# Sparse attention with two MLPs: all PSUM as one tile, softmax's maximum and difference over two banks, and split squares in fixed rooms of SBUF

## The chip, the cores and the metric

The kernel runs on one core of one Trainium2 chip. The metric is the device time of one execution in microseconds; lower is better. Three executions of the kernel before took 823.47, 827.84 and 828.2 us (median 827.84).

## The reference

Attention over 4 batches, 8 heads, 576 positions and a head size of 64, in float32. Four heads see only the last 32 positions (local), the other four see every 32nd position (strided). Its result, 2304 tokens by 512 channels, goes through two MLPs with an inner size of 2048.

```python
scores = scale * q @ k.T                      # masked: local for h < 4, strided for h >= 4
attn = exp(scores - max(scores)); attn /= sum(attn) + 1e-9
x = (attn @ v).transpose(0, 2, 1, 3).reshape(2304, 512)
h = x @ w_in;   x = (s * relu(h) ** 2 + b) @ w_out
h = x @ w_in2;  x = where(h >= 1, h, where(h <= -1, 0, (h + 1) ** 2 / 4)) @ w_out2
```

## The kernel before

Every float32 product of the MLPs is done with three matmuls of 384 columns on operands that are split into a high and a low part (`mm3`, lines 859 to 861, and `mm3s`, lines 1102 to 1104): high by high, high by low, low by high. The weights come from HBM in 8-byte words (`raw`, three buffers of 512 KB over 128 partitions), and `decode` and `weights` (L459 to L475) turn each into a high and a low half with two ScalarE and three VectorE or GpSimd operations.

The tokens are worked in six units of 384. Attention is cut into 21 tiles, 12 strided and 9 local ones (`attend`). A tile goes through these steps:

- TensorE writes scores into two PSUM banks (L737 to L757). For the first six tiles (`NACC`) these are two of the four banks named acc; later they are both banks named side.
- VectorE takes the maximum of each bank (L765, two instructions of 256 elements) and subtracts it from each bank (L768, two of 256). ScalarE takes the exponential (L771), VectorE the sum (L772) and its reciprocal (L773), and GpSimd or VectorE multiplies (L774).
- TensorE transposes four 128x128 blocks into a bank named h ("flip", L783); a copy brings them to SBUF as `pt`.
- TensorE multiplies by the values into both side banks (L799 for strided tiles, L809 for local ones). ScalarE moves each bank to the high half `xh` of x (L440), VectorE makes the low half `xl` of it (L842). A tile that crosses a unit's end is cut there, so that one bank takes two or more instructions.

Then, unit by unit, the first half of the first MLP's inner size: `hidden` multiplies `xh` and `xl` by the first weights into bank h, ScalarE and others take relu, the square `t` and its halves `gg`, and `output` multiplies these by the second weights into the four acc banks. The unit's partial sums go to HBM (`part`). The other half of the inner size and the second MLP follow pair of units by pair of units with seven products in place of eight (`product`, `hidden2`, `output2`); the prepared weight quarters go out to HBM from `prepare` and come back as `w0h`, `kb` and others.

No order is written by hand. Every step is recorded as an `Op` with a cost, and `Issue.order` draws 96 orders from the due times plus random jitter (`DRAWS`, `JITTER`) and keeps the one whose end is earliest by its own costs. `AHEAD` is how much earlier than due attention's later tiles are put. The same planner fills expected idle time of TensorE in the first 45 us with throwaway matmuls of 512 bf16 columns ("fills", L731), so many as `busy` is told:

```python
def busy(e, o, out):
    for _ in range(o.fills):
        e.matmul(out=out, lhsT=warm_t[:, 0:out.shape[0]], rhs=warm_t[:, 0:out.shape[1]], start=True, stop=True)
```

Storage is handed out by rings: PSUM tags h (2 banks), side (2) and acc0 to acc3 (1 each); SBUF tags such as `gg` (3 buffers of high and low half side by side), `t` (2) and `pi` (4). The rows of early attention tiles sit in x's tiles of units that are not open yet (`homes`).

Of the kernel before, what the change touches and what calls it, by code (L numbers as in the profile page):

```python
# [24 lines left out]
UMAX = max(UNITS)  # L25
GW = 2 * UMAX + 16
# [14 lines left out]
AHEAD = 3.0  # L41
# [10 lines left out]
PAIRS = NT // (2 * NP)  # L52
KP = DFF // 256
# [51 lines left out]
class Ring:  # L105
    def __init__(self, bufs):
        self.bufs, self.taken, self.made = bufs, [], []
# [220 lines left out]
def sparse_attention_two_mlps(ctx: ExitStack, tc: tile.TileContext, loc, strd, w_ins, w_outs, fixed, out):  # L328
# [17 lines left out]
    part_d = [dr.tile([KD, 128, n], F32, name=f"part_{u}") for u, n in enumerate(UNITS)]  # L346
# [10 lines left out]

    def home(tag):
        ring = rings.setdefault(tag, Ring(1))
        ring.name = tag  # L360
        serial[0] += 1
        name = f"{tag}_{serial[0]}"
        return Buf(ring, lambda: const.tile([128, KD * UMAX], F32, name=name, tag=tag))

    class Tokens:
        def __init__(self, tag):
            self.tag, self.bufs = tag, {}

        def open(self, u):
            tag, n = f"{self.tag}{u}", UNITS[u]  # L370
            ring = rings.setdefault(tag, Ring(1))
            ring.name = tag
            self.bufs[u] = Buf(ring, lambda: const.tile([128, KD, n], F32R, name=tag, tag=tag))
            return self.bufs[u]

        def __getitem__(self, u):
            return self.bufs[u].tile

    xh, xl, opened = Tokens("xh"), Tokens("xl"), {}
# [10 lines left out]

    def split_bufs(z):

        hi = buf(sp, "gg", [128, GW], F32R, LAG + 1)
        whole = hi.make

        def upper():
            hi.both = whole()
            return hi.both[:, UMAX:UMAX + z]

        hi.make = upper  # L400
        ring = rings.setdefault("gl", Ring(LAG + 1))
        ring.name = "gl"
        return hi, Buf(ring, lambda: hi.both[:, 0:UMAX])

    def wide_bank(tag, bufs, shape):
        b = buf(ps, tag, [128, 512], F32, bufs)
        whole = b.make

        def part():
            b.bank = whole()  # L410
            return b.bank[:, 0:shape[0] * shape[1]].rearrange("p (a b) -> p a b", a=shape[0])

        b.make = part
        return b
# [180 lines left out]
    def rows(i):  # L595
# [22 lines left out]
        if i in homes:  # L618
# [7 lines left out]
            else:  # L626
                for j in range(2):
                    load(i, both, [(lambda j=j: row()[:, j], strd[b, 2 * d + j][:, 0:VC])], 128 * VC * 4, 4 * VC)
# [801 lines left out]
```

## Time and profile before

| | |
|---|---|
| three executions | 823.47, 827.84, 828.2 us |
| profiled execution: its time, its span | 825.62 us, 823.7 us |
| TensorE busy | 811.2 us, 98% of the span |
| weight loads, VectorE, ScalarE, GpSimd busy | 785.3, 624.5, 515.1, 109.8 us |
| mean granted TensorE clock | 0.995 of 2.4 GHz |
| moved by DMA | 218.23 MB, 265 GB/s on average |

A matmul's row shows its time from entering to leaving the array, and matmuls overlap; the pace is read from the number of them in a stretch, and a stall from TensorE's idle time. The views used below are the table by stretches, the waits, the groups of instructions and the timeline.

### The profile page before, as it was taken

The page shows a single profiled execution, that of the slowest core. Times are in us where ns is not written, and L with a number is a line of the kernel's source. Part 1 is how long each engine was busy: PE and PEld are TensorE (multiplying, and loading weights), DVE is VectorE, ACT ScalarE, POOL GpSimd, SP SyncE. Part 2 cuts the span into 40 slices and gives each one's busy share as a digit, 9 for nine tenths or more (in the row PEclk, how much of TensorE's full clock was granted, in tenths as well). Part 3 has the DMA queues.
Part 4 walks back from the last instruction along what each step waited for, and adds up shares of the span by engine and source line. Part 5 has one row for each costly group of instructions (what it writes and reads, how often), then busy time and mean ns, then how long its engine had stood idle before and what let it go on. Part 6 is the DMA issues. An engine that isn't in the chain of part 4 may idle for free.

```text
span 823.7 us, 17684 instructions
## 1 busy us (share of the span) xinstructions
PE 811.2 (98%) x6301; PEld 785.3 (95%) x6301; DVE 624.5 (76%) x1314; ACT 515.1 (63%) x1052; POOL 109.8 (13%) x213
## 2 busy tenths in 40 slices
PE   7999999999999999999999999999999999999998
PEld 3689999998999999999999999999999999999998
DVE  4878438887867478679889987997477987466966
ACT  2577446555656566558676677855486855667553
POOL 4032104342321013030221010000000000000000
PEclk9999999999999999999999999999999999999999
DMA  7796355888777468899989999788988889878882
GB/s 230 259 294 203 113 178 196 301 293 288 266 263 253 157 244 279 287 313 341 338 320 326 308 397 342 255 252 281 300 253 255 254 251 294 288 254 253 250 271 95
DMA packets 105523, 218.23 MB, mean 265 GB/s; under 512 B 14196, under 2 KB 27868, under 8 KB 105436
## 3 DMA queue, kind: packets, MB, share of 16 engines
q1 hardware_dynamic: 95196, 180.41, 67.5%
q0 software_dynamic: 10240, 36.71, 11.9%
q8 instruction: 50, 0.82, 0.4%
q14 instruction: 37, 0.30, 0.1%
HBM read 170.93 MB, written 46.14 MB: 264 GB/s over the span
## 4 chain that ended last, share of the span: by engine, by line
PE 96%; DMA 2%; SPq 1%; DVE 0%; ACT 0%; issue 0%; POOL 0%; ACTq 0%
PE acc L1104 8%; PE acc L1103 8%; PE acc L1102 8%; PE h L859 8%; PE h L861 8%; PE h L860 8%; PE side L1104 6%; PE side L1102 6%; PE side L1103 6%; PE acc L859 4%; PE acc L861 4%; PE acc L860 4%; PE h L1104 3%; PE h L1103 3%; PE h L1102 3%; PE side L809 1%
## 5 line engine op out<-in xcount | busy, mean ns | idle before, releaser
L859 PE MATMUL h<-xh,w0h 128*128 128x384 f32 x192 | 65.7, 342 | 0.0
L859 PE MATMUL h<-xh,w0hx 128*128 128x384 f32 x192 | 65.6, 342 | 0.0
L861 PE MATMUL h<-xh,w0lx 128*128 128x384 f32 x192 | 64.6, 337 | 1.0 <-POOL w0lx L475 0.7
L860 PE MATMUL h<-xl,w0hx 128*128 128x384 f32 x192 | 64.4, 336 | 0.0
L860 PE MATMUL h<-xl,w0h 128*128 128x384 f32 x192 | 64.4, 336 | 0.0
L861 PE MATMUL h<-xh,w0l 128*128 128x384 f32 x192 | 64.4, 336 | 0.0
L505 POOL DMA_DIRECT2D dw<-pp x60 | 43.4, 723 | 157.6 <-DVE pp L503 131.0
L886 ACT ACTIVATE t<-h 128x384 f32<-128x384 f32 x50 | 24.5, 489 | 46.6 <-PE h L861 46.3
L898 DVE TENSOR_TENSOR gg<-t,gg 128x384 fp32r<-128x384 f32 x36 | 20.0, 555 | 26.7 <-ACT gg L440 26.7
L861 PEld LDWEIGHTS h<-xh,w0lx 128*128 128x128 f32 x192 | 36.0, 188 | 1.6 <-POOL w0lx L475 1.0
L859 PEld LDWEIGHTS h<-xh,w0h 128*128 128x128 f32 x192 | 36.0, 188 | 0.5
L859 PEld LDWEIGHTS h<-xh,w0hx 128*128 128x128 f32 x192 | 36.0, 188 | 0.5
L860 PEld LDWEIGHTS h<-xl,w0h 128*128 128x128 f32 x192 | 36.1, 188 | 0.0
L860 PEld LDWEIGHTS h<-xl,w0hx 128*128 128x128 f32 x192 | 36.1, 188 | 0.0
L861 PEld LDWEIGHTS h<-xh,w0l 128*128 128x128 f32 x192 | 36.0, 188 | 0.0
L440 ACT ACTIVATE gg<-w1h 128x384 fp32r<-128x384 f32 x48 | 24.9, 523 | 15.9 <-PE acc L1104 6.2
L1148 DVE TENSOR_TENSOR gg<-w1h,gg 128x384 fp32r<-128x384 f32 x48 | 26.5, 556 | 10.5 <-ACT gg L440 10.2
L859 PE MATMUL acc<-gg,w1h 128*128 128x384 f32 (+1 forms) x96 | 33.4, 348 | 0.0
L859 PE MATMUL acc<-gg,w1hx 128*128 128x384 f32 (+1 forms) x96 | 32.6, 340 | 0.0
L861 PE MATMUL acc<-gg,w1l 128*128 128x384 f32 (+1 forms) x96 | 32.3, 336 | 0.0
L861 PE MATMUL acc<-gg,w1lx 128*128 128x384 f32 (+1 forms) x96 | 32.2, 336 | 0.0
L860 PE MATMUL acc<-gg,w1h 128*128 128x384 f32 x96 | 32.2, 335 | 0.0
(607 smaller groups left out, 2804.8 us busy)
## 6 DMA issues: line engine op xcount, KB each, us to landing
dw<-pp POOLq DMA_DIRECT2D x60, 512.0 KB, 5.2
w0h<-dw SPq DMA_DIRECT2D x84, 256.0 KB
w0l<-dw SPq DMA_DIRECT2D x84, 256.0 KB
w0hx<-dw SPq DMA_DIRECT2D x84, 256.0 KB
w0lx<-dw SPq DMA_DIRECT2D x84, 256.0 KB
raw<-in_w_ins SPq DMA_DIRECT2D x32, 512.0 KB
raw<-in_w_outs SPq DMA_DIRECT2D x32, 512.0 KB
kb<-dw SPq DMA_DIRECT2D x56, 256.0 KB
```

Of the source, the lines that this page charges most:

```text
L440: e.activation(out=out, in_=in_, func=AF.Copy)
L505: op(lambda e: e.dma_start(out=dw[o][i][qs].rearrange("q p w n -> p q (w n)"), in_=y.tile[:, 0:nq].bitcast(F32).rearrange("p q w n -> p q ...
L809: e.matmul(out=pv[blk].tile[half(par), hp, c:c + 32], lhsT=v4(pos)[half(blk), s, 2 * hp + par, :], rhs=pt.tile[half(blk), 2 * par + pos, r ...
L859: e.matmul(out=acc, lhsT=wh, rhs=ah, start=first, stop=False)
L860: e.matmul(out=acc[:, 0:al.shape[1]], lhsT=wh, rhs=al, start=False, stop=False)
L861: e.matmul(out=acc, lhsT=wl, rhs=ah, start=False, stop=last)
L886: op(lambda e: e.activation(out=c(t), in_=c(p), func=AF.Relu), [act(n)], [p], [t])
L898: op(lambda e: e.tensor_tensor(out=c(gl), in0=c(t), in1=c(gh).bitcast(F32), op=SUB), [pool(n)] + [dve2(n)], [t, gh], [gl])
L1102: e.matmul(out=dst, lhsT=wh, rhs=ah, start=opens and first, stop=False, skip_group_check=not opens)
L1103: e.matmul(out=dst[:, 0:al.shape[1]], lhsT=wh, rhs=al, start=False, stop=False, skip_group_check=not opens)
L1104: e.matmul(out=dst, lhsT=wl, rhs=ah, start=False, stop=last, skip_group_check=not opens)
L1148: op(lambda e, g=g, hi=hi, lo=lo: e.tensor_tensor(out=lo.tile[:, 0:n], in0=g.tile, in1=hi.tile[:, 0:n].bitcast(F32), op=SUB), [dve2(n)], [ ...
```

## The change

- All eight PSUM banks become one tile, `banks_t`; `bank` hands out banks of it in the same turns as before (acc0 to acc3 are banks 0 to 3, side 4 and 5, h 6 and 7).
- Since a tile's two score banks now lie side by side in one tile (`both`), the maximum is one instruction over two banks (512 elements), and so is the difference. For local tiles both value banks are moved out by one instruction per half.
- x is kept per pair of units and half of the channels ([128, 2, 768]) and not per unit ([128, 4, 384]). Attention's results are cut only where a pair ends. The second MLP's input is read back into these tiles when both units of a pair are done with theirs.
- The halves of the squares (`g_t`) and the squares and partial sums (`f_t`) are fixed rooms near the start of SBUF; before, `t`, `gg` and `pi` were rings near its end. All other tiles move up by 18,624 bytes or less.
- `AHEAD` goes from 3.0 to 4.0, one more tile (10) gets a home in x's tiles, some of the planner's costs are changed, and code for uneven units goes.

```diff
-AHEAD = 3.0
+AHEAD = 4.0
...
+    BANKS = {"acc0": [0], "acc1": [1], "acc2": [2], "acc3": [3], "side": [4, 5], "h": [6, 7]}
+    def bank(tag, *shape):
+        ring = ring_of(("bank", tag), len(BANKS[tag]))
+        def make():
+            b.at = BANKS[tag][ring.used % ring.bufs]
+            ring.used += 1
+            b.bank = banks_t[:, b.at, :]
...
+    def both(two, n):
+        assert two[1].at == two[0].at + 1
+        return banks_t[:, two[0].at:two[0].at + 2, 0:n]
+    def place_in(arena, key, places, n):
+        k = turns.get(key, 0)
+        turns[key] = k + 1
+        a = places[k % len(places)]
+        t = g_t if arena == "g" else f_t
+        b = Part(lambda: t[:, a:a + n])
+        old = [x for x in taken[arena] if x[0] < a + n and a < x[1]]
+        b.writers = list(dict.fromkeys(o for *_, x in old for o in (*x.writers, *x.readers)))
...
     def split_bufs(z):
+        return tuple(place_in("g", v, [i * GW + v * NP for i in range(LAG + 1)], n) for v, n in ((1, z), (0, NP)))
...
-        for par in range(2):
-            op(lambda e, par=par: e.tensor_reduce(out=mx.tile[:, 4 * par:4 * par + 4], in_=sc[par].tile, op=ALU.max,
-                                                  axis=mybir.AxisListType.X), [dve(256)], [sc[par]], part=[mx])
-        for par in range(2):
-            op(lambda e, par=par: e.tensor_tensor(out=fours(2 * par, 2 * par + 2), in0=sc[par].tile.rearrange("p (a b) n -> p a b n", b=2),
-                                                  in1=each(2 * par, 2 * par + 2), op=SUB), [dve(256)], [sc[par], mx], part=[full])
+        op(lambda e: e.tensor_reduce(out=mx.tile.rearrange("p (c a) -> p c a", c=2), in_=both(sc, 256).rearrange("p c (a n) -> p c a n", n=64),
+                                     op=ALU.max, axis=mybir.AxisListType.X), [dve(512)], sc, part=[mx])
+        op(lambda e: e.tensor_tensor(out=sm().rearrange("p (c a) (b n) -> p c a b n", c=2, b=2),
+                                     in0=both(sc, 256).rearrange("p c (a b n) -> p c a b n", a=2, b=2),
+                                     in1=mx.tile.rearrange("p (c a b) -> p c a b", c=2, a=2).unsqueeze(4).to_broadcast([128, 2, 2, 2, 64]),
+                                     op=SUB), [dve(512)], [*sc, mx], part=[full])
...
+            moved_out([(lambda: both(pv, 256).rearrange("p c (h s q) -> p h s c q", h=2, s=4),
+                        lambda w: x_of(w, off, end).rearrange("p h (s c q) -> p h s c q", c=2, q=32))], pv, 512, 0.00104)
...
-        for u in us:
-            begun = op(lambda e: None, [("none", 0.0, 0.0)], after=[x_last[u]], allocs=[x2[u]])
+        begun = op(lambda e: None, [("none", 0.0, 0.0)], after=[x_last[u] for u in us], allocs=[x2[p, 0], x2[p, 1]])
```

How the order moves, at three places. First VectorE, its first instructions after the set-up of constants: the maximum (TENSOR_REDUCE mx from a bank) and the difference (TENSOR_TENSOR sm) of the first two tiles, the sum (mx from sm) and the reciprocal. Before:

```order
L765 TENSOR_REDUCE mx_201<-acc_17_199 128x4
L765 TENSOR_REDUCE mx_201<-acc_16_198 128x4
L768 TENSOR_TENSOR sm_200<-acc_16_198,mx_201 128x2x128
L768 TENSOR_TENSOR sm_200<-acc_17_199,mx_201 128x2x128
L765 TENSOR_REDUCE mx_235<-acc_25_233 128x4
L765 TENSOR_REDUCE mx_235<-acc_24_232 128x4
L772 TENSOR_REDUCE mx_201<-sm_200 128x8
L768 TENSOR_TENSOR sm_234<-acc_24_232,mx_235 128x2x128
L768 TENSOR_TENSOR sm_234<-acc_25_233,mx_235 128x2x128
L773 RECIPROCAL mx_201<-mx_201 128x8
```

The same place in the changed kernel:

```order
L785 TENSOR_REDUCE mx_187<-banks_t 128x8
L787 TENSOR_TENSOR sm_186<-banks_t,mx_187 128x4x128
L785 TENSOR_REDUCE mx_218<-banks_t 128x8
L793 TENSOR_REDUCE mx_187<-sm_186 128x8
L787 TENSOR_TENSOR sm_217<-banks_t,mx_218 128x4x128
L794 RECIPROCAL mx_187<-mx_187 128x8
L795 TENSOR_TENSOR sm_186<-sm_186,mx_187 128x4x128
```

Each pair has become one instruction; their sequence is otherwise kept.

Second TensorE, around the scores of the first local tile (number 3, whose rows come in last among those of the first tokens). Before, behind the last of its score matmuls (L757) stand tile 1's flip (L783) and then tile 0's values (L799, alternately into the two side banks):

```order
L757 MATMUL acc_40_338<-xl_9_281 32x64
L757 MATMUL acc_41_339<-xl_9_281 32x64
L783 MATMUL h_384<-id_t,sm_234 128x128 x4
L799 MATMUL side_392<-pt_323,w0hx_195 64x54 x2
L799 MATMUL side_393<-pt_323,w0hx_195 64x54 x2
```

In the changed kernel tile 0's values (L820) stand behind tile 2's scores (L763) and ahead of the local tile's, which begin with the mask (L758):

```order
L763 MATMUL banks_t<-k_4_206,q_5_209 54x54 x2
L763 MATMUL banks_t<-k_4_206,q_5_209 36x36 x2
L763 MATMUL banks_t<-k_4_206,q_5_209 54x54 x6
L820 MATMUL banks_t<-pt_271,w0hx_183 64x54 x16
L758 LDWEIGHTS idb_t
L758 MATMUL banks_t<-bias_t,idb_t 128x256
```

The values of tile 0 have moved from behind the first local tile's scores to ahead of them.

Third TensorE, after the first matmuls of `hidden` on unit 0. Before, 24 of them (two blocks of 128 inner values) are followed by three fills (the last is shown here), tile 5's flip, four more fills (the first is shown) and tile 5's values:

```order
L731 LDWEIGHTS warm_t
L731 MATMUL h_815<-warm_t 128x512
L783 MATMUL h_815<-id_t,sx_703 128x128 x4
L731 LDWEIGHTS warm_t
L731 MATMUL side_835<-warm_t 128x512
```

In the changed kernel 33 of them stand ahead of that flip (the last is the first row here), three behind it, and then two fills (the first is shown) and the values:

```order
L868 MATMUL banks_t<-xh_166,w0l_473 128x384
L804 MATMUL banks_t<-id_t,sx_629 128x128 x4
L866 MATMUL banks_t<-xh_166,w0h_472 128x384
L867 MATMUL banks_t<-xl_167,w0h_472 128x384
L868 MATMUL banks_t<-xh_166,w0l_473 128x384
L752 LDWEIGHTS warm_t
L752 MATMUL banks_t<-warm_t 128x512
```

A third block of `hidden` has moved ahead of tile 5's values, and five fills are gone there. Over the whole program TensorE has 46 fills and not 53, VectorE 1,236 instructions and not 1,316, ScalarE 1,040 and not 1,054; the 4,248 matmuls of 384 or 386 columns and attention's other matmuls are as many as before. From the end of attention on, TensorE's matmuls come in the same sequence of blocks in both.

## Rows read from the trace of the kernel before

**Rows 1.** Cores: span and mean granted TensorE clock, of full speed.

```profile
core 0: 823.7 us, clock 0.995
```

**Rows 2.** Stretches: length; PE, weight loads, DVE, ACT, POOL busy; clock; DMA share; GB/s.

```profile
0.00:37.46 37.46, 30.72 (x588) 18.09 (x588) 22.81 (x65) 14.11 (x36) 10.08 (x45) 0.91 0.75 244
37.46:44.86 7.40, 7.40 (x107) 6.22 (x100) 6.80 (x15) 4.84 (x10) 1.83 (x2) 1.00 0.98 301
44.86:80.00 35.14, 34.14 (x355) 31.34 (x350) 29.64 (x69) 26.75 (x62) 11.73 (x20) 1.00 0.83 254
80.00:220.00 140.00, 138.75 (x1817) 130.04 (x1816) 95.88 (x239) 77.11 (x172) 41.78 (x76) 1.00 0.67 226
220.00:480.00 260.00, 260.00 (x1493) 259.66 (x1492) 205.15 (x419) 171.40 (x337) 41.64 (x67) 1.00 0.83 289
...
520.00:820.20 300.20, 300.20 (x1730) 299.90 (x1728) 228.91 (x439) 188.66 (x374) 0.00 (x0) 1.00 0.81 255
820.20:823.74 3.54, 0.02 (x1) 0.00 (x0) 0.56 (x1) 0.03 (x1) 0.00 (x0) 0.86 0.31 111
```

**Rows 3.** TensorE's waits: us in total, times, longest; 0 to 45, then after.

```profile
PE acc L757 <- DMA xh<-in_loc: 2.3, 1, 2.3
PE acc L757 <- DMA xl<-in_loc: 1.9, 1, 1.9
PE side L731 <- DVE xl L842: 0.8, 1, 0.8
...
PE h L783 <- issue: 1.2, 1, 1.2
```

**Rows 4.** Groups on VectorE by shape: busy us, mean ns, idle before.

```profile
L765 DVE TENSOR_REDUCE mx<-side 128x4 f32<-128x256 f32 x30 | 11.4, 417 | 8.0 <-PE side L757 4.7 <-PE side L742 3.3
L772 DVE TENSOR_REDUCE mx<-sm 128x8 f32<-128x520 f32 x14 | 9.7, 690 | 0.9 <-ACT sm L771 0.8
```

**Rows 5.** Timeline, 8 to 38 us: start, duration, engine, line, instruction, count.

```profile
8.67 1.90 PE L731 MATMUL acc<-warm_t 128*128 128x512 bf16 x8
8.84 0.76 DVE L765 TENSOR_REDUCE mx<-acc 128x4 f32<-128x256 f32 x2
...
19.20 1.12 PE L799 MATMUL side<-pt,w0hx 54*64 54x54 f32 x32
20.25 2.74 PE L731 MATMUL h<-warm_t 128*128 128x512 bf16 x6
...
30.91 0.66 ACT L440 ACTIVATE xh<-side 128x256 fp32r<-128x256 f32 x2 [1.40 <-PE side L809]
31.33 0.76 DVE L842 TENSOR_TENSOR xl<-side,xh 128x256 fp32r<-128x256 f32 x2 [0.66 <-ACT xh L440]
...
35.84 0.89 DVE L842 TENSOR_TENSOR xl<-side,xh 128x128 fp32r<-128x128 f32 x4 [0.29 <-ACT xh L440]
...
37.47 0.44 PE L859 MATMUL h<-xh,w0h 128*128 128x384 f32 x1
```

**Rows 6.** Timeline, 41.7 to 68.1 us, the same columns.

```profile
41.74 0.82 PE L731 MATMUL h<-warm_t 128*128 128x512 bf16 x3
42.40 0.60 PE L783 MATMUL h<-id_t,sx 128*128 128x128 f32 x4
42.84 1.03 PE L731 MATMUL side<-warm_t 128*128 128x512 bf16 x4
43.79 0.67 PE L809 MATMUL side<-pt,qx 64*64 64x32 f32 x32
...
44.86 0.44 PE L859 MATMUL h<-xh,w0h 128*128 128x384 f32 x1
...
61.63 0.44 PE L861 MATMUL h<-xh,w0lx 128*128 128x384 f32 x1 [0.32 <-DVE w0lx L475]
...
68.04 0.44 PE L861 MATMUL h<-xh,w0lx 128*128 128x384 f32 x1 [0.69 <-POOL w0lx L475]
```

More of the change, by code (lines that the diff above doesn't have):

```diff
@@ L720, in attend @@
         ahead = i < NACC
-        sc = [wide_bank(f"acc{i % 2 * 2 + par}" if ahead else "side", 1 if ahead else 2, [4, 64]) for par in range(2)]
+        sc = [bank(f"acc{i % 2 * 2 + par}" if ahead else "side", 4, 64) for par in range(2)]
         tag = ("sm", "sm", "sx")[i % 3]
@@ L789, in attend @@
         nv = 108 if strided else 128
-        pv = [wide_bank("side", 2, [2, nv]) for _ in range(2)]
+        pv = [bank("side", 2, nv) for _ in range(2)]
         def values(e, i=i):
@@ L870, in hidden @@
     def hidden(g, u, whole=None):
-        n = UNITS[u]
-        p = buf(ps, "h", [128, UMAX], F32, 2)
+        t0, n = (NP * u, NP) if whole else (U0[u], UNITS[u])
+        p, more = bank("h", n), 0
         if whole:
-            t, own = whole, [whole]
+            t = whole
         else:
-            t = buf(sp, "t", [128, UMAX], F32, TB)
             more = 2 * (u == COUNTED)
-            gh, gl = split_bufs(UMAX + more)
-            own = [t, gh, gl]
+            gh, gl = split_bufs(n + more)
+            t = square_buf()
         w = wt[g, 0]
         for k in range(KD):
-            pe_op(lambda e, k=k: mm3(e, p.tile[:, 0:n], cut(w, k), (xh[u][:, k, :], xl[u][:, k, :]), k == 0, k == KD - 1),
-                  n, [*w, x_buf[u][k]], [p], own if k == 0 else ())
-        x_last[u] = chain[0]
+            pe_op(lambda e, k=k: mm3(e, p.tile, cut(w, k), (x_at("h", k, t0, n), x_at("l", k, t0, n)), k == 0, k == KD - 1),
+                  n, [*w, *(x_buf[v][k] for v in range(NU) if t0 < U0[v + 1] and U0[v] < t0 + n)], [p], [whole] if whole and k == 0 and whole.ring else ())
+        if whole:
+            x_last[u] = chain[0]
         c = lambda b: b.tile[:, 0:n]
@@ L904, in units @@
     def units(hi, lo, n):
[L905 removed]
+        op(lambda e: copy(e, hi.tile[:, n:n + 2], ones_t[:, 0:2]), [("pool", 0.2, 0.1)], part=[hi], after=hi.writers)
     bias_sum = Buf(None, None)
@@ L930, in output @@
         z = n + 2 * (u == COUNTED)
[L931 to L937 removed]
+        gh, gl = gt
+        cg = lambda: (gh.tile[:, 0:z], gl.tile[:, 0:n])
         for c in range(KD):
             if opens:
[L940 removed]
+                acc[c] = bank(f"acc{c}", z)
             a = acc[c]
@@ L1002, in inputs @@
[L1002 to L1009 removed]
+            whose = [x2[p, int(place[1]) - 1]]
@@ new lines, in inputs @@
+            op(lambda e, place=place, b=b: copy(e, b.tile[:, 0], x(place)), [("act", 0.17 + 2 * NP * 0.00062, 0.1)], [quarter[p][place], *whose], [b],
+               after=[x_last[i // 2 * 2], x_last[i // 2 * 2 + 1], *(mixed if i < 2 else ())] if i < NB else plan.ops[begin:])
+            op(lambda e, place=place, b=b: e.tensor_tensor(out=b.tile[:, 1], in0=x(place), in1=b.tile[:, 0].bitcast(F32), op=SUB),
+               [("dve", 0.09 + 2 * NP * 0.00104, 0.1, "port")], [quarter[p][place], *whose], [b])
```

268 lines of the change are left out of this document (98 added, 170 removed).

## The prediction

> **What bounds the kernel now.** I read the cores first, then the table by stretches, TensorE's waits, the groups of VectorE and last the timeline where TensorE is not steady. TensorE's clock is granted at 0.995 of 2.4 GHz [rows 1], so little is to be had from the clock, save at the start, where the first stretch shows 0.91 [rows 2]. In that table the reader is to see that from 220 us to the end of the matmuls TensorE is busy in every microsecond (260.00 of 260.00, 300.20 of 300.20), while VectorE and ScalarE are at 60 to 80%. Whatever they save there is worth nothing. The pace is 300.20 / 1730 = 173.5 ns a matmul from 520 us on, and 260.00 / 1493 = 174.1 ns between 220 and 480 us [rows 2].
>
> TensorE's idle time sits in four places [rows 2]: 37.46 - 30.72 = 6.7 us ahead of the first `hidden` matmul, 1.0 us between 45 and 80 us, 1.25 us between 80 and 220 us, 3.5 us behind the last matmul (the last evacuation and the store). To these come the fills, busy but of no use: eight took 1.90 us and four 1.03 us, so one at full clock costs (1.90 - 1.03) / 4 = 0.22 us, but six at the lower clock took 2.74 us, 0.46 us each [rows 5, 6]. 53 of them are some 14 us. So the change can win at most about 25 us, nearly all of it in the first 45 us; what it can lose has no such bound.
>
> **The change part by part.**
>
> *Two banks at once.* A pair of maxima of 256 takes 0.76 us [rows 5], a single one 417 ns, and a sum over 520 elements 690 ns [rows 4]. So one instruction of 512 should take about 0.69 us and save 0.07 us; the same for the difference. Over 21 tiles that is 2 x 21 x 0.07 = 2.9 us of VectorE, and none of it on the path after 45 us, where TensorE covers it. At the start the chain of the last local tile before `hidden` gains 0.14 us. No row shows a VectorE instruction over two banks: from below it can't beat one of 417 ns, from above it might take two of them in full, 0.83 us. I take 0.69, the row of nearly the same length.
>
> *Local tiles moved out at once.* Before, VectorE began on the first bank 0.42 us after ScalarE did (30.91 and 31.33), and ended 1.18 us after ScalarE's start [rows 5]. In one piece it can begin only when ScalarE is through with both, 0.66 us or a little less, and then runs 0.69 us: 1.35 us, 0.17 us more. Where a unit's end cut the tile, four pieces took 0.89 us [rows 5] and become one of about 0.69. Together with the 0.14 us above I take 0 for the chain to the first `hidden`, between -0.3 and +0.3 us. Strided tiles lose cuts only.
>
> *One PSUM tile.* Each ring has as many banks and the same turns, so no bank is waited for that was not before. A two-bank instruction holds both banks until its end, but one TensorE step writes both anyway, and the next such step needs both.
>
> The Trainium skill speaks against this part in "PSUM — Partial Sum Buffer", section "PSUM bank collisions raise a hardware error": no two engines may touch one bank at a time, so it wants PSUM guarded by banks, and a two-bank read shuts both to all others for its whole length. In this kernel the trace shows one wait of TensorE for a side bank, 0.8 us [rows 3]; by that rule it would grow by at most the 0.27 us between 0.69 and 0.42.
>
> *The order at the start.* Tile 0's values, 1.12 us [rows 5], stood behind the first local tile's scores and now stand ahead of them, where TensorE waits 2.3 and 1.9 us for that tile's rows [rows 3]: they become free, -1.1 us. Between those scores and the first `hidden` there were 33 fills and are 32: -0.2 us. Less idle time there may also keep the clock up, so that fills cost 0.22 and not 0.46 us. Against this, the chain of VectorE and ScalarE may set the first `hidden`, and then nothing is won. I take -1.5 us for its start (37.47 us before [rows 5]), between -4 and +1.
>
> *The hole behind the first blocks.* From 41.74 to 44.86 us TensorE did three fills, a flip, four fills and tile 5's values [rows 6]. The fills were 0.82 + 1.03 = 1.85 us; two remain, 0.43 us. A third block of `hidden` does the covering: -1.4 us, between -2.0 and 0 (its weights might not be there in time).
>
> *What the weights take back.* At 61.6 and 68.0 us TensorE waits 0.32 and 0.69 us for the low half of a weight block [rows 6]; DMA is at 0.98 in the stretch to 45 us and 0.83 in the one behind it [rows 2]. So the weights of the first unit come just in time, and a TensorE that is 2.9 us earlier waits for them, unless they are decoded earlier too. I take half, +1.4 us, between 0 and +2.9.
>
> *The rest of attention.* The single wait of 1.2 us there ("issue", a flip) [rows 3] has no cause in the program that I can see and may stay, go or come twice: 0, between -1.25 and +1.25. `AHEAD` of 4.0 shifts where the 15 later tiles stand; a bad place is the slower rival below.
>
> *Pair-wise x.* The read-back waits for the second unit's last block, 12 matmuls or 2.1 us after the first's. The first sum that needs it comes a whole product of 48 matmuls, 8.3 us, later, so the wait is hidden; if it weren't, 2.1 us three times.
>
> *Rooms.* The split squares move some 180 KB down. If the 1493 matmuls at 174.1 ns came to 173.5, that is -0.9 us; if all 4,248 went from 173.5 to 174.1, +2.6 us. The two stretches differ in what else runs, and no row ties it to addresses, so I take 0.
>
> The sum is -1.5 - 1.4 + 1.4 = -1.5 us on the profiled execution's 825.62 us: 824.1, rounded to 824. That execution is 2.2 us below the median of the three shown, 827.84, and inside their spread, 823.47 to 828.2; a measurement of this kernel tells about 1%, 8.3 us, from no change.
>
> **The rivals.**
>
> *A, the whole start is won.* The first `hidden` starts 4 us earlier, the hole goes, and the decoding of the weights moves forward as well, so that the 1.0 us between 45 and 80 us goes too: 825.6 - 4.0 - 1.4 - 1.0 = 819.2. For it: the fills at 0.46 us, and DMA at 0.75 in the first stretch. Against: DMA at 0.98 right behind it.
>
> *B, the weights take all back.* 825.6 + 0 to 0.5: 826. For it: the two waits at 61.6 and 68.0 us.
>
> *C, slower: the side banks.* From tile 6 on, scores and values take both side banks in turn. In the new order three strided tiles of a batch have their scores 12 matmuls apart, 12 x 0.1735 = 2.1 us. Maximum and difference need 0.69 + 0.69 us, and with one other instruction of 0.69 ahead of them on VectorE, 2.07 us; a second one makes TensorE wait, and all that TensorE has queued behind the scores waits with it. At 0.8 us, the one such wait of before [rows 3], for each of the 15 tiles that is +12: 837.6. It decides from some 0.55 us a tile. Against it: before, there was a single such wait in 21 tiles, and VectorE, not TensorE, sat idle for scores (8.0 us [rows 4]).
>
> *D, the pace falls.* A fill's 512 columns take 0.217 us at full clock, so 384 would take 0.163 us; if the new distances freed the matmuls to that pace, 4,248 x 0.0107 = 45 us would go: 780. No stretch comes near it, whatever is read from where [rows 2].
>
> The Trainium skill, "TensorE: Matmul & The Clock Gate", section "Wait — 56ns, not 53.3ns?", gives columns over 2.4 GHz plus about 2.5 ns for a matmul at full clock, 162.5 ns for 384 columns, an estimate by that page. The trace agrees with it for the bf16 fills (217 ns) and disagrees for these fp32r matmuls (173.5 ns).
>
> **How the numbers follow.** The forecast has 0.64, A 0.14, B 0.13, C 0.07, D 0.02. Faster by over 1% of the median (below 819.6) is about half of A, since 819.2 lies at the line, with D and a little of the forecast's tail: 0.11. Slower by over 1% (above 836.1) is C and a little tail: 0.08. The rest, 0.81, is within 1%. The terms' own bounds add up to -0.3 - 4 - 2 - 1.25 - 0.9 = -8.5 at one end and 0.3 + 1 + 2.9 + 1.25 + 2.6 = +8.1 at the other, from 825.6: 817 and 834. I give 817 to 833, which holds the forecast, A and B and leaves out C and D.
>
> **What would show it.** Right: an instruction of L785 and L787 takes about 0.69 us; the first `hidden` matmul starts near 36 us and tile 5's values come within 44 us; TensorE's waits for w0l and w0lx between 45 and 80 us grow from 1.0 to about 2.4 us; 173 to 174 ns a matmul from 220 us on. Wrong: a first `hidden` before 34 or after 38.5 us, waits of TensorE for a side bank at several tiles, or a pace that moves by over 1 ns in a long stretch.

## The result, and the profile after

The changed kernel takes 831.04 us (median of 20 executions, 829.01 to 834.77), the kernel before beside it on the same chip 826.75 us (20 executions, 822.75 to 832.29). The ratio is 1.0057, with a 95% interval of 1.004 to 1.0075: slower by 4.7 us, between 3.3 and 6.2. That is within 1%, inside the predicted range of 817 to 833, and on the other side of no change than the forecast of 824.

The table by stretches of the changed kernel (columns as in [rows 2]; the first and the seventh row end where TensorE's first `hidden` matmul starts and where its last matmul ends):

```profile
0.00:36.57 36.57, 27.27 (x581) 16.03 (x586) 21.62 (x46) 12.11 (x23) 11.05 (x45) 1.00 0.74 233
36.57:44.86 8.29, 8.20 (x80) 7.46 (x74) 7.52 (x14) 6.52 (x13) 1.04 (x3) 1.00 0.97 246
44.86:90.00 45.14, 39.82 (x499) 35.63 (x498) 32.78 (x66) 28.10 (x65) 12.20 (x22) 1.00 0.71 216
90.00:220.00 130.00, 128.49 (x1687) 119.73 (x1664) 83.79 (x175) 72.74 (x156) 37.30 (x68) 1.00 0.69 229
220.00:480.00 260.00, 259.92 (x1488) 259.62 (x1488) 207.90 (x422) 171.41 (x335) 46.40 (x70) 1.00 0.82 284
480.00:525.00 45.00, 43.27 (x249) 42.64 (x248) 35.34 (x71) 35.55 (x74) 2.73 (x4) 1.00 1.00 370
525.00:828.90 303.90, 303.90 (x1744) 303.55 (x1742) 231.62 (x443) 189.64 (x375) 0.00 (x0) 1.00 0.80 254
```

Two stretches of the kernel before that [rows 2] cuts otherwise or leaves out, in the same view:

```profile
44.86:90.00 45.14, 44.14 (x471) 40.88 (x466) 34.23 (x79) 30.70 (x70) 13.62 (x23) 1.00 0.70 216
...
480.00:520.00 40.00, 40.00 (x233) 40.00 (x232) 34.77 (x70) 32.16 (x67) 2.73 (x4) 1.00 0.97 351
```

Read the first two numbers of each row against each other. Between 44.86 and 90 us TensorE now stands idle for 45.14 - 39.82 = 5.3 us, where it was 1.0; between 480 and 525 us for 1.7 us, where it was none. From 525 us on it is busy throughout, as before, but 303.90 / 1744 = 174.3 ns a matmul stand against 173.5 ns [rows 2]. These are the three places at which the time went. In this execution the clock is granted in full throughout, 1.00 in the first stretch too, where it was 0.91 in the profiled execution of the kernel before.

TensorE's waits in the changed kernel (answers to [rows 3]), of 0 to 45 us, then of 45 to 90, 90 to 220 and 480 to 835 us:

```profile
PE banks_t L778 <- DMA xl<-in_loc: 3.1, 2, 2.1
PE banks_t L763 <- DMA xl<-in_strd: 1.6, 1, 1.6
...
PE banks_t L820 <- ACT w0hx L461: 2.2, 1, 2.2
PE banks_t L820 <- ACT dt L480: 0.8, 1, 0.8
PE banks_t L866 <- ACT w0hx L461: 0.8, 1, 0.8
PE banks_t L868 <- POOL w1l L496: 0.7, 1, 0.7
PE banks_t L830 <- DMA qv<-in_loc: 0.7, 2, 0.5
...
PE banks_t L868 <- issue: 1.4, 1, 1.4
...
PE banks_t L1070 <- ACT w1l L1057: 1.5, 1, 1.5
```

L820 is the values of a strided tile. Its wait of 2.2 us is the largest between 45 and 90 us, and it has no counterpart in the kernel before. The timeline of the changed kernel from 61 to 74 us shows where it comes from (start, duration, engine, line, instruction; in brackets the idle time before it; SPq is the queue that issues the loads):

```profile
61.12 0.35 SPq L476 DMA_DIRECT2D raw<-in_w_outs  x1
...
63.94 0.34 SPq L476 DMA_DIRECT2D raw<-in_w_ins  x1
...
68.10 0.55 PE L763 MATMUL banks_t<-k,q 64*36 64x36 f32 x24
...
69.20 0.67 ACT L480 ACTIVATE dt<-raw 128x512 f32<-128x512 f32 x1 [1.00 <-DMA raw<-in_w_ins]
...
69.91 0.43 DVE L482 TENSOR_SCALAR dt<-dt 128x512 int32<-128x512 int32 x1 [0.59 <-ACT dt L480]
...
70.43 0.69 DVE L496 TENSOR_TENSOR w1lx<-dt,w1hx 128x512 fp32r<-128x512 f32 x1
...
71.04 0.69 DVE L785 TENSOR_REDUCE mx<-banks_t 128x8 f32<-128x512 f32 x1
...
71.28 0.67 ACT L480 ACTIVATE dt<-raw 128x512 f32<-128x512 f32 x1 [0.88 <-DMA raw<-in_w_outs]
...
71.64 0.68 DVE L484 SCALAR_TENSOR_TENSOR dt<-raw,dt 128x512 int32<-128x512 int32 x1
71.84 0.59 ACT L461 ACTIVATE pt<-banks_t 128x512 f32<-128x512 f32 x1
72.24 0.69 DVE L787 TENSOR_TENSOR sx<-banks_t,mx 128x512 f32<-128x512 f32 x1
...
73.03 0.69 PE L820 MATMUL banks_t<-pt,qx 54*64 54x54 f32 x32 [2.23 <-ACT w0hx L461]
```

The words of a weight block (`raw`) are asked for at 63.94 us and ScalarE, which is to decode them, waits for them until 69.20. VectorE waits for ScalarE, and behind the decoding (L482, L496, L484) stand the maximum and the difference of tile 8, whose scores (L763) have lain in the two side banks since 68.65. The difference ends at 72.24 + 0.69 = 72.93, and only then have the values of tile 7, which go into the same banks, a place: 73.03. Their other operand, the copy `pt` of tile 7's transposed block, stands on ScalarE behind one more decoding that waits for words (0.88 us) and ends at 71.84 + 0.59 = 72.43, so that it holds them up nearly as long. The wait is put down to `w0hx`, which ended at the same moment and is no operand of the values.

The view by tile, here of `raw` from 36 to 90 us, sums up what its readers waited for (us, times), in the changed kernel:

```profile
its engine sat idle before it (us, times) until:
  DMA raw<-in_w_ins: 4.6, 3
  DMA raw<-in_w_outs: 3.8, 6
```

and in the kernel before:

```profile
its engine sat idle before it (us, times) until:
  DMA raw<-in_w_outs: 1.9, 2
```

The load that is issued at 63.94 us in the changed kernel is the 13th of words; in the kernel before the 13th goes out 2.9 us earlier:

```profile
61.04 1.06 SPq L455 DMA_DIRECT2D raw<-in_w_ins  x1
```

The second place, near 487 us, looks different. The timeline of the changed kernel:

```profile
475.45 0.73 POOL L526 DMA_DIRECT2D dw<-pp  x1 [31.09 <-ACT pp L461]
476.69 0.72 POOL L526 DMA_DIRECT2D dw<-pp  x1 [0.51 <-DVE pp L524]
...
483.54 0.49 ACT L461 ACTIVATE pp<-banks_t 128x384 f32<-128x384 f32 x1 [3.33 <-DMA dw<-pp]
...
486.91 0.41 PE L1070 MATMUL banks_t<-tm,w0l 128*128 128x384 f32 x1 [1.50 <-ACT w1l L1057]
```

and of the kernel before:

```profile
440.06 0.72 POOL L505 DMA_DIRECT2D dw<-pp  x1 [2.06 <-issue]
...
475.62 0.49 ACT L440 ACTIVATE pp<-side 128x384 f32<-128x384 f32 x1 [0.42 <-PE side L1104]
485.66 0.71 POOL L505 DMA_DIRECT2D dw<-pp  x1 [1.43 <-DVE pp L503]
```

A buffer `pp`, from which prepared weights are stored, takes a product's bank when the second MLP begins. Before, the last store from it had begun 35 us ahead of that. In the changed order two stores have come to stand there, and ScalarE waits 3.3 us for one to land. TensorE then waits 0.2 us for the product's bank and 1.5 us until an instruction that stands behind `pp` on ScalarE (L1057) is done. This is read from one trace and was not tried by an experiment. In nine other traces with this order, or nearly so, ScalarE waits for a store from `pp` too, 2.4 to 5.4 us, but TensorE's wait there (1.0 to 1.4 us each) ends in five of them with an instruction of ScalarE and in four with the load of a weight, `w0l<-dw`. So the order makes this loss, as the experiments below show, and by which of its steps stays open.

The merged maximum and difference take what was forecast (groups on VectorE, answers to [rows 4]):

```profile
L785 DVE TENSOR_REDUCE mx<-banks_t 128x8 f32<-128x512 f32 x21 | 14.5, 690 | 25.8 <-PE banks_t L763 13.2 <-PE banks_t L778 12.5
...
L787 DVE TENSOR_TENSOR sm<-banks_t,mx 128x512 f32<-128x512 f32 x14 | 9.6, 689 | 0.7
```

### The profile page after: what moved, and what is told of

Read it like the earlier page. It is cut to its first block, busy times and chain, and to the rows that moved or that the text cites. A ratio compares the mean times of both kernels' runs of the same rounds, so it can differ in the third digit from the quotient of the medians.

```text
span 832.6 us, 17521 instructions
## 1 busy us (share of the span) xinstructions
PE 810.9 (97%) x6288; PEld 784.7 (94%) x6294; DVE 621.1 (75%) x1234; ACT 516.1 (62%) x1038; POOL 110.7 (13%) x211
## 4 chain that ended last, share of the span: by engine, by line
PE 85%; DMA 9%; issue 4%; ACT 1%; SPq 1%; DVE 0%; ACTq 0%; POOLq 0%
PE banks_t L1070 16%; PE banks_t L1072 16%; PE banks_t L1071 16%; PE banks_t L866 12%; PE banks_t L868 11%; PE banks_t L867 11%; DMA raw<-in_w_outs 4%; DMA xh<-in_loc 1%; DMA dw<-pp 1%; PE banks_t L830 1%; PE banks_t L804 1%; DMA w0hx<-in_strd 1%; SPq L605 1%; PE banks_t L778 1%; DMA w0lx<-in_loc 1%
## 5 line engine op out<-in xcount | busy, mean ns | idle before, releaser
L866 PE MATMUL banks_t<-xh,w0hx 128*128 128x384 f32 x192 | 65.4, 341 | 0.8 <-ACT w0hx L461 0.8
L868 PE MATMUL banks_t<-xh,w0lx 128*128 128x384 f32 x192 | 64.7, 337 | 1.5 <-issue 1.4
L866 PE MATMUL banks_t<-xh,w0h 128*128 128x384 f32 x192 | 65.8, 343 | 0.1
L868 PE MATMUL banks_t<-xh,w0l 128*128 128x384 f32 x192 | 64.5, 336 | 0.0
L867 PE MATMUL banks_t<-xl,w0h 128*128 128x384 f32 x192 | 64.4, 336 | 0.0
L867 PE MATMUL banks_t<-xl,w0hx 128*128 128x384 f32 x192 | 64.4, 335 | 0.0
L461 ACT ACTIVATE g_t<-f_t 128x384 fp32r<-128x384 f32 x78 | 40.5, 521 | 11.1 <-PE banks_t L1072 10.0
L867 PEld LDWEIGHTS banks_t<-xl,w0h 128*128 128x128 f32 x192 | 36.1, 188 | 0.0
L867 PEld LDWEIGHTS banks_t<-xl,w0hx 128*128 128x128 f32 x192 | 36.1, 188 | 0.0
L868 PEld LDWEIGHTS banks_t<-xh,w0l 128*128 128x128 f32 x192 | 36.1, 188 | 0.0
```

What stands on the lines that cost most here:

```text
L461: e.activation(out=out, in_=in_, func=AF.Copy)
L866: e.matmul(out=acc, lhsT=wh, rhs=ah, start=first, stop=False)
L867: e.matmul(out=acc[:, 0:al.shape[1]], lhsT=wh, rhs=al, start=False, stop=False)
L868: e.matmul(out=acc, lhsT=wl, rhs=ah, start=False, stop=last)
```

## The experiments

Theory 1: the order of the steps, which the planner drew anew, makes the loss. Theory 2: the rooms, from which TensorE reads the split squares, make it. Theory 3: the instructions over two banks or the shared PSUM tile make it. The first two experiments cross order and instructions: the order that the planner gave to the one kernel is written into the other as a table.

### The changed instructions in the order before, and the reverse

```diff
-        return min((self.draw(seed) for seed in range(DRAWS)), key=lambda x: x[0])[1]
+        rows = json.loads(zlib.decompress(base64.b85decode(ORDER)))
+        return {o: (float(t), names[e], k) for o, (t, e, k) in zip(self.ops, rows)}
```

In the kernel with the changed instructions tile 10 also loses its home in x's tiles; in the other one it gets one.

> The changed kernel with its merged instructions, its one PSUM tile, its pair-wise x and its rooms, but every step put where the kernel before has it, with the same fills on TensorE (a step that has become one of two stands where the first or the last of them stood; tile 10's rows go to the buffers they had before; the read-backs of x stand at most 3.4 planned us later, behind the second unit's last block). Theory 1, the order alone makes the loss of 4.7 us: 826.7 us or up to 1 less, TensorE's waits between 45 and 90 us near 1.0 us in sum and not 5.2, matmul number 192 near 82.4 us. Theory 2, the rooms: it keeps the 1.5 us that the changed kernel loses in pace from 490 us on, 828.3. Theory 3, the merged instructions or the shared PSUM tile: it keeps all, 831.

Measured: ratio to the kernel before 1.0018 (1.0 to 1.0036), +1.5 us. TensorE's idle time from 44.86 to 90 us is 0.9 us, and matmul number 192 of those with 384 or 386 columns starts at 82.44.

> The kernel before with its single-bank instructions and its old places in SBUF, put in the changed kernel's order with its fills (tile 10's rows in x's tiles as there, and the square takes its buffer when it is written). Theory 1, the order: 830 to 831 us, with some 5 us of waits on TensorE between 45 and 90 us and the wait of 1.5 us near 487 us. Theory 2, the rooms: 829.5 at most, since the pace stays at 173.5 ns from 520 us on. Theory 3, the merged instructions: 826.7.

Measured: 1.0049 (1.0029 to 1.0068), +4.0 us (2.4 to 5.6), and matmul 192 at 89.22 us; in this profiled execution the first `hidden` matmul was late as well, at 40.15 us, with a granted clock of 0.87 up to there. TensorE's waits from 45 to 90 us are 3.3 us and not 5, and hold the one of 2 us before the values:

```profile
PE side L809 <- ACT pt L450: 2.1, 1, 2.1
```

So the order by itself, with the old instructions and the old places, costs most of the loss, and the changed kernel in the old order loses 1.5 us, which is what theory 2 leaves to the rooms. Theory 3 had both numbers the other way round.

### The rooms

```diff
-    g_t = const.tile([128, (LAG + 1) * GW], F32R, name="g_t")
-    f_t = const.tile([128, (KD + TB) * NP], F32, name="f_t")
+    g_t = last.tile([128, (LAG + 1) * GW], F32R, name="g_t")
+    f_t = last.tile([128, (KD + TB) * NP], F32, name="f_t")
```

`last` is a pool that stands behind all others in SBUF.

> The changed kernel, its order and instructions untouched, with the rooms for the split squares, the squares and the partial sums behind everything else in SBUF and not near its start; weights and x stand where they stood before the change. Theory 2, the rooms: the matmuls that read split squares fall from 175.1 to 174.0 ns and the time by 1.3 to 1.5 us, to 829.5. Theories 1 and 3: 831, with the same waits on TensorE.

Measured: 1.0034 (1.0014 to 1.0053) in place of 1.0057, 1.9 us less, though the two intervals overlap. To see which rooms and why there, four kernels moved them apart; one profiled execution of each gives the pace, so single times are not compared.

```diff
-    g_t = const.tile(
+    g_t = last.tile(
```

> The changed kernel with only the split squares' rooms at the end of SBUF, the squares and partial sums left near its start. If the place of what TensorE reads is what counts: 173.6 ns a matmul from 530 us on, 1,247 matmuls in 216.5 us between numbers 3000 and 4247. If it is the squares and partial sums, which only the other engines and DMAs touch: 174.3 ns, 217.4 us.

```diff
-    f_t = const.tile(
+    f_t = last.tile(
```

> The changed kernel with only the squares' and partial sums' rooms at the end of SBUF, the split squares left at the very bytes where the change puts them, and weights and x 9.2 KB lower. If the place of the split squares counts, near SBUF's start: 174.3 ns a matmul from 530 us on, 217.4 us between numbers 3000 and 4247. If it is their exact distance from the weights, it may come out at any pace between 173.6 and 175. If it is the squares and sums: 173.6 ns.

In the next two a pool `mid` holds `g_t`, once behind the weights' pool and once ahead of it.

> The changed kernel with the split squares directly behind all weights, at bytes 166,240 to 175,648 of a partition. If a place above the weights is what counts: 173.6 ns a matmul from 530 us on, as with the rooms at the very end. If only the end of SBUF is good: 174.3.

> The changed kernel with the split squares directly in front of the weights, at bytes 100,704 to 110,112, while the weights stand where the change has them. If standing below the weights is what costs: 174.3 ns a matmul from 530 us on. If it is the start of SBUF: 173.6.

Measured: the stretch from matmul 3000 to matmul 4247 (of the 4,248 with 384 or 386 columns), whose length is the first number behind the two times. The changed kernel, and then the kernels with only `g_t` at the end, only `f_t` at the end, `g_t` behind the weights and `g_t` ahead of them:

```profile
611.18:828.58 217.40, 217.40 (x1249) 217.40 (x1248) 164.18 (x316) 135.79 (x270) 0.00 (x0) 1.00 0.78 249
```

```profile
603.85:820.24 216.39, 216.39 (x1248) 216.39 (x1248) 163.79 (x316) 135.78 (x270) 0.00 (x0) 1.00 0.79 249
```

```profile
610.14:827.53 217.39, 217.39 (x1249) 217.39 (x1248) 164.16 (x316) 135.74 (x270) 0.00 (x0) 1.00 0.78 248
```

```profile
606.84:823.25 216.41, 216.41 (x1249) 216.41 (x1248) 163.77 (x316) 135.77 (x270) 0.00 (x0) 1.00 0.80 250
```

```profile
608.31:824.96 216.65, 216.65 (x1249) 216.65 (x1248) 163.92 (x316) 135.80 (x270) 0.00 (x0) 1.00 0.80 249
```

It is the split squares alone that count. Above the weights they give 173.5 ns a matmul, at SBUF's start 174.3, right ahead of the weights in between, 173.7 (from 217.40, 216.39 and 216.65 us over 1,247 matmuls): the place matters, and not only whether it is above or below the weights. The kernel before takes 216.42 us there. The rooms' whole price, counted from matmul 864 to 2000 (198.24 against 198.00 us) and from 2500 to 4247 (304.48 against 303.21), is 1.5 us.

### The merged instructions

```diff
+        op(lambda e: [e.tensor_reduce(out=mx.tile[:, 4 * c:4 * c + 4], in_=sc[c].tile, op=ALU.max, axis=mybir.AxisListType.X)
+                      for c in range(2)], [dve(512)], sc, part=[mx])
```

The difference is split in the same manner.

> The changed kernel in its own order with the maximum and the difference done again by two instructions of one bank each, which stand behind each other where the merged one stood. Theory 3, that an instruction over two banks holds TensorE up: the waits between 60 and 90 us fall by 2 us or more and the time goes to 829 or below. Theories 1 and 2: 831, and 0.07 us more of VectorE per pair, 2.9 us in all, that TensorE covers.

Measured: 1.0075 (1.006 to 1.009). TensorE's idle time from 44.86 to 90 us was 2.7 us in its trace, not 5.3, but the wait of 2 us before the values is in it, and in the other traces with the merged form in this order the idle time is 3.0 to 4.3 us. The single-bank form is at least not faster, so that part of theory 3 falls; the shared PSUM tile is still in this kernel. The first and the third experiment together leave the merged instructions, the one PSUM tile and the pair-wise x in the old order and with good rooms:

> The first experiment's kernel (the changed instructions in the order of the kernel before) with the rooms behind everything else in SBUF as in the third: what is left of the change is the merged instructions, the one PSUM tile and the pair-wise x. If order and rooms are all that costs: 826 us, level with the kernel before or up to 1 us faster, 173.6 ns a matmul from 530 us on. If the merged instructions hold something up that the order hid: 827 or more.

Measured: 0.9981 (0.9964 to 0.9999), -1.6 us (-3.0 to -0.1). It is the one kernel of this study that is ahead of the kernel before, by little more than can be told. So neither the merged instructions nor the one PSUM tile make the loss.

### Is it the weights' words?

```diff
+        few = DM // cut_
+        words = lambda i: raw.tile.rearrange("p (a b) -> p a b", b=2)[:, 0:few, i].unsqueeze(1).to_broadcast([128, cut_, few])
-        load = op(lambda e: e.dma_start(out=raw.tile.bitcast(I64), in_=src), [dma(
+        load = op(lambda e: e.dma_start(out=raw.tile.bitcast(I64)[:, 0:few], in_=src[:, 0:few]), [dma(
```

> The changed kernel in its own order, with only half of the 8-byte words fetched for the weight blocks 7 to 16 of the first half of the first MLP (256 of 512 columns; the decoding reads those twice, so it does as many instructions of the same length, and the results of that MLP are not the reference's). Theory 1a, the order makes the words land late, so that ScalarE stands at their decoding with softmax's steps queued behind it: ScalarE's waits for them between 36 and 90 us fall from 8.4 to under 2.5 us, TensorE's waits between 45 and 90 us from 5.2 to under 2.5 us, matmul number 192 comes 2.5 to 4 us earlier (near 84 us) and the time is 827 to 828.5. Theory 1b, it is the sequence of instructions on VectorE and ScalarE itself, whatever lands when: 831 and the same waits on TensorE.

> The kernel before, in its own order, with the same half of the words fetched as in the fifth experiment (the first MLP's results are not the reference's). Theory 1a: it gains at most its own 1.0 us of waits for words in the stretch, so 825.5 to 826.5, and the changed kernel's 2.6 us are the order's. If half the words help any order alike: 2 us or more, 824.5 or less.

Measured: 1.0025 (1.0004 to 1.0046) in place of 1.0057 in the changed order, and 0.9987 (0.9968 to 1.0006) in the order before: 2.6 us against 1.1 us. The intervals alone do not part these two gains; the traces do. The stretch from 44.86 to 90 us in the changed order with half the words, and in the order before:

```profile
44.86:90.00 45.14, 43.40 (x620) 39.72 (x614) 36.65 (x73) 31.07 (x71) 14.28 (x23) 1.00 0.50 155
```

```profile
44.86:90.00 45.14, 44.81 (x499) 41.53 (x492) 34.07 (x80) 31.14 (x71) 13.36 (x23) 1.00 0.53 165
```

In the changed order TensorE's idle time falls from 5.3 to 1.7 us and no reader of `raw` waits for a DMA; in the order before it falls from 1.0 to 0.3. From the first `hidden` matmul to matmul 864, when attention is over, the two orders now take 192.5 and 192.3 us; with all words it was 199.5 and 194.0, or 196.6 and 193.7 in the means of the table below. With the words in time the orders are level there. Theory 1a holds, 1b does not. What the two runs do not part is the words' own landing from that of the other loads on the same queue, which half the words may also let go earlier.

```diff
-tile 8: maximum at 63.71, difference at 64.96; tile 7: copy at 64.51
+tile 8: maximum at 62.50, difference at 62.51; tile 7: copy at 63.92
```

These are planned times in the written order, and nothing else is moved.

> The changed kernel in its own order but for three instructions: tile 8's maximum and difference stand ahead of a decoding on VectorE, and the copy of tile 7's transposed block ahead of one on ScalarE, near 70 us. If TensorE's wait of 2.2 us for the values at 73 us is softmax queued behind decoding that waits for words: that wait falls under 0.7 us and the time by 1 to 2 us, to 829 to 830, unless the decoding that is now later asks 1 us or more of it back. If the wait is set by something else (the rows of the values, the side banks' turn): it stays at 2 us and the time at 831.

Measured: 1.0048 (1.002 to 1.0077). TensorE's waits there:

```profile
PE banks_t L878 <- POOL w1l L506: 0.7, 1, 0.7
PE banks_t L814 <- POOL sx L805: 0.7, 1, 0.7
PE banks_t L830 <- ACT pt L471: 0.4, 1, 0.4
PE banks_t L830 <- issue: 0.2, 1, 0.2
```

The wait before the values (L830 here) has gone from 2.2 us (2.0 to 2.9 in the seven traces of the changed order below) to 0.6 us, so it was softmax behind the decoding; which of the three instructions counted most was not tried apart. A new wait of 0.7 us and one of 1.4 us after 90 us, with 10 matmuls at half the clock behind it, took most of it back, and the time is not told from the changed kernel's.

### What made the order

```diff
-AHEAD = 4.0
+AHEAD = 3.0
```

> The changed kernel with AHEAD of 3.0 in place of 4.0, so that its planner draws another order from the same costs. If AHEAD of 4.0 is what makes the order worse: 827 to 828.3 (the rooms' 1.5 us stay), with waits of TensorE near 1 us between 45 and 90 us. If it is the planner's new costs or the luck of the draw: anything from 827 to 833, and no nearer to the kernel before than another draw.

> The kernel before with AHEAD of 4.0 in place of 3.0 and nothing else. If AHEAD is what makes the order worse: 829 to 831, with 4 us or more of waits on TensorE between 45 and 90 us. If it is luck or the other costs: within 1.5 us of 826.5.

```diff
-        return min((self.draw(seed) for seed in range(DRAWS)), key=lambda x: x[0])[1]
+        return min((self.draw(seed) for seed in range(1000, 1000 + DRAWS)), key=lambda x: x[0])[1]
```

> The changed kernel with 96 other random draws (numbers 1000 to 1095 in place of 0 to 95), all costs and AHEAD as they are. If the costs or AHEAD make its orders bad: 830 to 833 again, with some 5 us of waits on TensorE between 45 and 90 us. If it is the luck of one draw: a different time by 2 us or more, as likely below 829 as above, and waits elsewhere.

Measured: 1.0032 (1.0014 to 1.005), 1.0001 (0.998 to 1.0022) and 1.002 (0.9999 to 1.0041). AHEAD is not shown to be it: in the kernel before it makes another order (TensorE idle for 2.8 us from 44.86 to 90 us in its trace, not 1.0, but the first `hidden` matmul at 35.28 us) that takes the same time. Other draws from the very same costs give back 3 us, and what is left to them is about the rooms' 1.5. So, as far as two other orders for the changed kernel show, the order was a bad draw, with costs that do not see it: the planner took it for the best of 96.

```diff
-        late = RAW_LAG if raw else 0.0
+        late = RAW_LAG if raw else 3.0
```

> The changed kernel with its rooms at the end and a planner that takes the words of the first MLP's first half to land 3 us later than it did, so that its order has softmax's steps ahead of decodings whose words are not there. If the unmodelled landing is what makes its orders bad: ScalarE's waits for words between 36 and 90 us under 4 us, TensorE's waits between 45 and 90 us under 3 us, and 824 to 827. If a draw's luck outweighs it: 827 to 830.

Measured: 1.0074 (1.005 to 1.0099), with good rooms: the worst order of all. The readers' waits for words fell to 1.3 us, as expected, but TensorE's waits between 45 and 90 us came to 4.9 us, the scores waiting for rows and `hidden` for weights that are now decoded late. My remedy was wrong.

### The traces side by side

Times in us. First: start of the first `hidden` matmul. Then the length from it to matmul 864 and TensorE's idle time in it, and the lengths from matmul 2232 to 2500 and from 3000 to 4247, each counted in the trace of one execution.

| kernel | order | first | to 864 | idle | 2232 to 2500 | 3000 to 4247 |
|---|---|---|---|---|---|---|
| before | before | 37.47 | 194.0 | 2.2 | 46.5 | 216.42 |
| changed, old order | before | 37.39 | 193.1 | 1.0 | 46.5 | 217.39 |
| the same, rooms at the end | before | 36.34 | 193.9 | 1.8 | 46.5 | 216.39 |
| changed | changed | 36.58 | 199.5 | 6.9 | 48.8 | 217.40 |
| before, changed order | changed | 40.15 | 195.6 | 3.3 | 48.5 | 216.41 |
| rooms at the end | changed | 35.63 | 195.9 | 4.4 | 48.0 | 216.39 |
| single banks | changed | 35.62 | 196.1 | 4.7 | 48.2 | 217.39 |
| only split squares at the end | changed | 35.14 | 195.2 | 3.3 | 48.3 | 216.39 |
| only squares and sums at the end | changed | 37.72 | 196.1 | 3.9 | 49.6 | 217.39 |
| split squares behind the weights | changed | 36.94 | 195.6 | 3.3 | 48.2 | 216.41 |
| split squares ahead of the weights | changed | 35.90 | 197.8 | 5.4 | 48.6 | 216.65 |

The three rows in the old order have a mean of 37.1 us for the first matmul, 193.7 to matmul 864 with 1.7 idle, and 46.5. The seven rows of changed instructions in the changed order have 36.2, 196.6 with 4.6 idle, and 48.5. So the changed order wins 0.9 us at the start, loses 2.9 in attention, all of it idle time of TensorE, and 2.0 where the second MLP begins; with the rooms' 1.5 that is 5.5, against 4.7 (3.3 to 6.2) measured. The 0.9 us at the start are not clear of the scatter: in one and the same order the first matmul came between 35.14 and 37.72 us, and at 40.15 us with the old instructions. The profiled execution of the changed kernel is the slowest of its order in attention, which is why the two spans lie 8.9 us apart.

That the 2.9 us are as much as the idle time grew hides two things that nearly cancel: five fills less (1.1 us), and TensorE's clock (0.9 us in the mean of the seven). In four of the seven traces, and in that of the old instructions in this order, the granted clock falls from 1.00 to 0.50, 1.2 of 2.4 GHz, right behind the long wait before the values. The kernel with only the split squares at the end, from 70 to 73 and from 74 to 77 us:

```profile
70.00:73.00 3.00, 3.00 (x11) 3.00 (x10) 3.00 (x9) 2.29 (x6) 2.36 (x2) 0.50 0.75 217
74.00:77.00 3.00, 3.00 (x39) 2.72 (x39) 1.10 (x3) 1.91 (x5) 0.00 (x0) 1.00 0.14 52
```

There TensorE stood idle for 2.87 us up to 67.99 us, and from 69.8 us on 11 matmuls start 0.32 us apart and not 0.17, which costs some 1.6 us. In the other three traces, the changed kernel's own among them, the wait was 2.0 to 2.2 us and the clock stayed at 1.00; with the old instructions it fell after 2.15 us.

## Why the prediction was wrong

*Two banks at once.* Right: 690 and 689 ns. That it is hidden is right too; if anything it wins (-1.6 us with the pair-wise x, in the old order).

*Local tiles moved out at once, one PSUM tile.* Right as far as seen: no wait that these would make stands in the trace of the kernel with the merged instructions in the old order and the rooms at the end. The Trainium skill, "PSUM — Partial Sum Buffer", section "PSUM bank collisions raise a hardware error", had spoken against the shared read; no run here shows that it cost time.

*The order at the start.* Forecast -1.5 us and a first matmul near 36 us; it came at 36.58, and at 36.2 in the mean of seven, -0.9, with a scatter between executions as large as that.

*The hole.* Forecast -1.4, with two fills in place of seven. Five fills went as said, and 24 matmuls after the first one TensorE was 4 us ahead (40.85 against 44.86), 0.9 us of it from the start. Tile 5's values began at 43.92, within the 44 us, but one of their operands landed late (0.7 us of waits for `qv`, L830 above) and the block after it, the fourth, began at 46.49. Before, the fourth block began at 47.05, so that 0.6 us of the 4 were left.

*What the weights take back.* This is the step that failed. The prediction said that "a TensorE that is 2.9 us earlier waits for them, unless they are decoded earlier too. I take half, +1.4 us, between 0 and +2.9." Its bound assumed that the words land when they landed before. But SP's queue is ordered by the same draw, and the prediction goes by the orders of TensorE and VectorE only. The 12th load of words is issued at 61.12 us, behind loads of rows, though VectorE had read the buffer that it goes to by 57.39; before, it was issued at 60.07, 0.5 us after that. The 13th load of words is issued at 63.94 us where it was 61.04. In both kernels it goes out as soon as VectorE has read the 10th block's buffer, at 63.85 and at 60.98, so a block that comes late makes the third one behind it late too. And the waits were looked for at the weights' own matmuls (0.8 and 0.7 us there), while the larger ones came at the values, through softmax queued behind the decoding. The term was put at +1.4, at most +2.9; it measured some +4, with what the slower clock and the rest of attention took: 2.9 us lost from the first matmul to number 864, though the hole's 1.1 us of fills are won in it. With half the words the loss there was gone (192.5 against 192.3 us). In that stretch VectorE stood idle for 0.59 us before L482 while the scores for its maximum, behind it, had been ready for 0.7 us.

*The rest of attention.* Forecast 0 (±1.25): the wait put down to "issue" was 1.4 us in the profiled execution in place of 1.2. Of the seven traces in the changed order three have it (1.4 to 1.9 us) and four do not, of the three in the old order one: it comes and goes with executions.

*Rival C.* It named the side banks and a price of 0.8 us a tile for 15 tiles. The place was right and the mechanism half: not the tiles' closeness but decoding that waits on VectorE, at two tiles (0.8 and 2.2 us) and not 15. Its price of 12 us was far too high.

*Pair-wise x.* Right: the same trace shows no wait for the read-back. The loss of 2.0 us near 487 us appears with the old instructions in the changed order too (48.5 us), and had no term of its own in the prediction; of its cause only the late ScalarE behind the stores from `pp` and, in some traces, a late load are seen. The prediction took the order as unchanged there, since TensorE's blocks keep their sequence after attention; the stores from `pp` do not keep their place.

*Rooms.* Forecast 0 (-0.9 to +2.6), as "no row ties it to addresses". It is +1.5, inside the bounds; the value was wrong. That the pace from 220 us on would be 173 to 174 ns was wrong as well: 259.92 / 1488 = 174.7 ns between 220 and 480 us and 174.3 from 525 us on.

*The others.* Rival D did not come. Of rival A the early start came in part and was lost again, as B said; but B ended level with the kernel before, and the loss went on past that.

*The sum.* From -1.5 to +4.7 us are 6.2 us. The weights were put 2.6 us too low, the place near 487 us at nothing (2.0), the rooms at nothing (1.5), and the start and the hole 0.6 and 0.3 us too favourably. That makes 7.0, which agrees with 6.2 within the interval of the measured time.

## What to carry to other kernels

Where a planner draws the whole order, a small edit is also a new draw, worth some 3 to 4 us here, and the way to tell the two apart is to run the new instructions in the old order and the old ones in the new. When a gain is said to be limited by what lands when, the queue that issues the loads and the buffers that they wait for have to be compared as well, for they move too; and waits are to be looked for at everything that is queued behind the late consumer, not at its own matmul.

## What was not expected of the hardware

The place of a moving operand in SBUF changes TensorE's pace by 0.4%: 174.3 ns a matmul of 384 fp32r columns with the split squares at the start of SBUF, 173.7 directly ahead of the weights, 173.5 above them, the same within 0.1 ns in all 18 traces of this study, whatever the order. The Trainium skill, "SBUF — State Buffer", section "SBUF: two separate sides", says that TensorE never waits on anyone at its ports to SBUF. No trace here shows another engine that it would wait for, and the pace depends on the place all the same; the cause stays open.

A load of 512 KB of words took 5.3 us from its issue to its reader's start when the reader was waiting for it (63.94 to 69.20), and the next one 4.8 us (66.48 to 71.28).

TensorE's clock fell to half in the middle of attention: after a wait of 2.1 to 2.9 us in five traces of the changed order, but not after waits of 2.0 to 2.2 us in three others. In a loss that is read as waiting, some 1.6 us can therefore be matmuls at the lower clock.
